# One load queue in place of two, and a rearranged token mixer, in a lightning-attention kernel on one core

## The chip, the cores and the metric

The kernel runs on one core of a Trainium2 chip. The metric is the device time of one execution in microseconds (us), and I quote medians of several executions. A ratio is the mean time of one kernel's fast runs over the mean of the other kernel's fast runs of the same rounds on the same chip, so it is not quite the ratio of the two medians. An execution over 1.5% above the fastest of the same kernel counts as slow and is left out of ratios. The profile is of one execution; its span is 1.7 us (after) to 2.0 us (before) shorter than the time of that execution (119.18 and 129.39 us). The kernel before was run again beside every experiment, with medians of 127.45 to 129.03 us, so a difference below 1% between runs of different rounds says nothing by itself.

The engines are TensorE (PE for matmuls, PEld for its weight loads), VectorE (DVE), ScalarE (ACT), GpSimd (POOL) and SyncE (SP), which here only issues DMAs.

## The reference

Four batches of eight heads, 768 positions, head width 64. First a causal linear attention with a decay per head, then a token mixer with a hidden width of 64:

```python
# per head, blocks of 64 positions
intra = (qb @ kb.T) * Dmask;  out = intra @ vb + (qb * lam_pow) @ kv_state
kv_state = lam_block * kv_state + (kb * rev_pow).T @ vb
# x: [4, 768, 512], the heads side by side
wq = x @ w_q;  wk = x @ w_k                # 512 -> 64 each
W_tok = (wq @ wk.T) / sqrt(64)
out = maximum(W_tok @ x, 0) @ w_out        # 512 -> 512
```

The kernel takes the mixer as wq @ (wk.T @ x), so no 768 x 768 matrix is made.

## The kernel before

It works on 16 pairs of heads, four pairs a batch. For a pair it loads q, k and v, scales v by a decay (GpSimd, tile `vn`), transposes q and k on TensorE (`turn`, tiles `trq` and `trk`), makes states (`dps`), scores (`sc`), the share from the states and the values (`oa`). A batch's mixer runs during the pairs of the next batch. Its first product is `pq`, the transposes for the second are `pk`, the second `py`, the third `pm` with the ReLU in its eviction (the copy of a result out of PSUM, the memory that TensorE's products are written to; tile `rmT`), and the output product `po`.

The loads: k and q are cast to bf16 by DMAs that GpSimd issues, v comes as f32 by SP.

```python
def load_kv(n):
    t = stage.tile([128, 2, NCH, D], F32, tag="fv", name="fv")
    nc.sync.dma_start(out=t, in_=v[...])
    t = stage.tile([128, 2, NCH, D], BF16, tag="fk", name="fk")
    nc.gpsimd.dma_start(out=t, in_=k[...])
# load_q: likewise, nc.gpsimd, BF16
```

The loop (AHEAD = 7, pools of nine stage buffers a tile):

```python
for n in range(N):
    load_kv(n + AHEAD); load_q(n + AHEAD)
    cast(n + 2)                      # GpSimd: vn = v * decay
    if n == 1: cast_weights()        # GpSimd
    scores(n)
    # mixer of batch b-1: mix_pk at kk 1, mix_pm(half 0) at kk 2, mix_pm(half 1) at kk 3
    turn(n + 1); flip(n - 1)
    # mix_pq at kk 0, mix_py at kk 1; two output tiles in kk 2 and 3, one in kk 0 and 1
    inter(n); values(n); states(n + 1)
```

GpSimd takes its instructions in program order, and these are both the scaling and the issuing of loads.

Of the kernel before, what the change touches and what calls it, by code (L numbers as in the profile page):

```python
# [22 lines left out]
AHEAD = 7  # L23
# [3 lines left out]
def kernel(  # L27
# [15 lines left out]
    nat = ctx.enter_context(tc.tile_pool(name="nat", bufs=3))  # L43
    tsb = ctx.enter_context(tc.tile_pool(name="tsb", bufs=3))
# [16 lines left out]

    def load_q(n):
        b, kk = pairs[n]
        t = stage.tile([128, 2, 3, 2 * D], BF16, tag="fq", name="fq")
        nc.gpsimd.dma_start(  # L65
            out=t,
            in_=q[b, 2 * kk : 2 * kk + 2].rearrange("h (a p r) d -> p h a (r d)", p=128, r=2),
        )
        staged[n, "q"] = t

    def load_kv(n):
        b, kk = pairs[n]
        t = stage.tile([128, 2, NCH, D], F32, tag="fv", name="fv")
        nc.sync.dma_start(
            out=t, in_=v[b, 2 * kk : 2 * kk + 2].rearrange("h (c p) d -> p h c d", p=128)
        )
        staged[n, "v"] = t
        t = stage.tile([128, 2, NCH, D], BF16, tag="fk", name="fk")
        nc.gpsimd.dma_start(  # L79
            out=t, in_=k[b, 2 * kk : 2 * kk + 2].rearrange("h (c p) d -> p h c d", p=128)  # L80
        )
        staged[n, "k"] = t

    lam_all = consts.tile([128, H], F32, name="lam_all")
    nc.sync.dma_start(out=lam_all, in_=lam.partition_broadcast(128))
    load_kv(0)
    load_q(0)
    load_kv(1)


# [18 lines left out]
    )  # L109
    lnl = consts.tile([128, H], F32, name="lnl")  # L110
# [16 lines left out]
    Dq = []  # L127
    for kk in range(NP):
        t = consts.tile([128, S], BF16, name=f"dq{kk}")
        nc.scalar.activation(out=t, in_=ET, func=ACT.Exp, scale=lncol[:, kk : kk + 1])  # L130
        Dq.append(t)
    maskc = consts.tile([128, 3, CH], BF16, name="maskc")

    def build_mask():
        nc.gpsimd.memset(maskc, 1.0)
        nc.gpsimd.affine_select(
            out=maskc.rearrange("j c (r p) -> j c r p", r=2),
            in_=maskc.rearrange("j c (r p) -> j c r p", r=2),
            compare_op=ALU.is_ge,
            fill=0.0,  # L140
            base=0,
            pattern=[[0, 3], [1, 2], [2, 64]],
            channel_multiplier=-1,
        )

    wqk_f = consts.tile([128, 4, 2 * DHY], F32, name="wqk_f")
    wqk = consts.tile([128, 4, 2 * DHY], BF16, name="wqk")
    wo_f = consts.tile([128, 4, HD], F32, name="wo_f")
    wo = consts.tile([128, 4, HD], BF16, name="wo")

    def load_weights():
        nc.sync.dma_start(
            out=wqk_f[:, :, 0:DHY], in_=moe_w_q.rearrange("(kt p) j -> p kt j", p=128)
        )
        nc.sync.dma_start(
            out=wqk_f[:, :, DHY:], in_=moe_w_k.rearrange("(kt p) j -> p kt j", p=128)
        )
        nc.sync.dma_start(out=wo_f, in_=moe_w_out.rearrange("(kt p) j -> p kt j", p=128))

    def cast_weights():  # L160
        nc.gpsimd.tensor_scalar_mul(
            out=wqk[:, :, 0:DHY], in0=wqk_f[:, :, 0:DHY], scalar1=1.0 / 8.0
        )
        nc.gpsimd.tensor_copy(out=wqk[:, :, DHY:], in_=wqk_f[:, :, DHY:])
        nc.gpsimd.tensor_copy(out=wo, in_=wo_f)
# [5 lines left out]
    def cast(n):  # L171
        b, kk = pairs[n]
        fk, fv = staged.pop((n, "k")), staged.pop((n, "v"))
        kn = fk
# [130 lines left out]
    def flip(n):  # L305
# [4 lines left out]
        nc.vector.tensor_copy(out=xnat[b][:, :, kk * CH : (kk + 1) * CH], in_=xp)  # L310


    M = {}

    def mix_pq(b):
        qkT = hyp.tile([128, S], BF16, tag="qkT", name="qkT")
# [159 lines left out]
```

## Time and profile before

| | before |
|---|---|
| median (first 3 runs) | 128.13 us (127.66 to 128.55) |
| span of the profiled execution | 127.4 us |
| states of pair 4 start | 43.35 us |
| one steady batch (pairs 8 to 11) | 22.2 us |
| tail after the last pair | 18.5 us (108.9 to 127.4) |

Besides the lines that the prediction shows, more readings matter. First the page itself: busy time of each engine, then the DMA issues (count, KB each, median us from issue to landing).

```profile
span 127.4 us, 3311 instructions
PE 94.8 (74%) x1382; PEld 63.3 (50%) x1392; DVE 54.8 (43%) x119; ACT 66.9 (53%) x123; POOL 59.3 (47%) x61
...
fv<-in_v_dram SPq DMA_DIRECT2D x16, 384.0 KB, 14.4
...
fk<-in_k_dram POOLq DMA_DIRECT2D x16, 192.0 KB, 20.2
fq<-in_q_dram POOLq DMA_DIRECT2D x16, 192.0 KB, 20.2
```

No engine is full over the whole span, and a load takes 14 to 20 us to land, five to seven times the 2.95 us that TensorE needs for a pair without mixer work.

Then the waits of the kernel before (engine, tile and line; what it waited for; us in total, times, longest):

```profile
PE trq L191 <- DMA fq<-in_q_dram: 16.4, 3, 9.8
...
POOL fk L79 <- DMA fk<-in_k_dram: 9.9, 7, 2.8
...
PE dps L223 <- POOL vn L176: 8.1, 3, 4.6
...
PE py L344 <- DVE wkn L338: 2.6, 3, 0.9
```

TensorE loses 24.5 us to q that has not landed and v that is not scaled. The mixer's own wait is 2.6.

Last the DMA view of 20 to 25 us (packets of each queue; q0 is GpSimd's, q1 SP's):

```profile
DMA packets 3802, 0.82 MB, mean 164 GB/s; under 512 B 3801, under 2 KB 3801, under 8 KB 3801
...
q0 software_dynamic: 1923, 0.33, 81.5%
q1 hardware_dynamic: 1878, 0.48, 72.4%
```

The two queues get equal numbers of packets in these 5 us, 760 a us together (over 10 to 45 us it is 15366 and 11683, with SP at times having less asked for). But a pair needs 2304 rows of q and k (q0) and only 1536 of v (q1), so with equal turns v runs ahead of the q and k that it is useless without: v of pair 5 lands at 33.6 us, its q at 39.5.

### The profile page before, as it was taken

The numbers are of one execution on the slowest core, as the hardware profiler recorded it, in microseconds if no ns is written. First come the engines' busy times: TensorE is split into PE (matmuls) and PEld (weight loads), VectorE is DVE, ScalarE is ACT, GpSimd is POOL, SyncE is SP. The second block draws the span as 40 slices with busy tenths as digits, with TensorE's granted clock in tenths as the row PEclk, the third lists the DMA queues.
The fourth block names the chain that finished last, engine by engine and source line by source line (L and its number), as shares of the span: only waits on it lengthen the run. The fifth ranks groups of instructions, "written<-read, shape, count | busy, mean of one in ns | idle before, by whom it ended". The sixth has DMA issues, their size and how long they took to land.

```text
span 127.4 us, 3311 instructions
## 1 busy us (share of the span) xinstructions
PE 94.8 (74%) x1382; PEld 63.3 (50%) x1392; DVE 54.8 (43%) x119; ACT 66.9 (53%) x123; POOL 59.3 (47%) x61
## 2 busy tenths in 40 slices
PE   0008290650986399799999799999979999899970
PEld 0007280530874376568586556658655665434420
DVE  0103626110658090938855919385491936110000
ACT  4292050140055025369867449786744978647970
POOL 6999963237499956675848574314040000000000
PEclk9999999555599658999999999999999999999999
DMA  2999999999999999999999999998020240424284
GB/s 44 214 166 215 215 308 167 163 164 164 162 163 165 163 164 164 163 165 164 163 163 165 182 237 206 217 219 210 16 87 0 82 153 24 157 86 161 87 331 165
DMA packets 67407, 20.41 MB, mean 160 GB/s; under 512 B 63808, under 2 KB 63808, under 8 KB 67392
## 3 DMA queue, kind: packets, MB, share of 16 engines
q0 software_dynamic: 37376, 6.29, 62.6%
q1 hardware_dynamic: 30016, 13.90, 52.5%
q8 instruction: 11, 0.18, 0.5%
q14 instruction: 4, 0.03, 0.1%
HBM read 20.19 MB, written 6.29 MB: 208 GB/s over the span
## 4 chain that ended last, share of the span: by engine, by line
PE 54%; POOL 18%; DMA 16%; DVE 4%; issue 4%; ACT 2%; POOLq 0%; ACTq 0%
PE po L373 14%; DMA fk<-in_k_dram 14%; POOL fk L79 5%; PE pq L321 5%; POOL vn L176 5%; PE py L344 5%; PE sc L245 4%; PE dps L223 4%; PE oa L289 4%; PE pm L359 4%; POOL fq L65 4%; PE oa L268 4%; PE xp L309 4%; DVE pr L257 4%; PE trq L191 3%
## 5 line engine op out<-in xcount | busy, mean ns | idle before, releaser
L257 DVE TENSOR_TENSOR pr<-sc,maskc 128x384 bf16<-128x384 f32 x64 | 31.1, 548 | 0.2 <-PE sc L245 0.2
L210 ACT COPY kT<-trk 128x768 bf16<-128x768 bf16 x16 | 12.9, 809 | 31.4 <-PE trk L206 31.4
L176 POOL TENSOR_TENSOR vn<-fv,DvI 128x768 bf16<-128x768 f32 x16 | 23.7, 1482 | 12.3 <-PE oa L289 8.5
L232 DVE CAST gs<-dps 128x320 bf16<-128x320 f32 x16 | 7.9, 492 | 37.0 <-PE dps L223 37.0
L373 PE MATMUL po<-wo,rmT 128*128 128x512 bf16 x86 | 22.5, 380 | 0.6 <-issue 0.2
L191 PE MATMUL trq<-ident,fq 128*64 128x128 bf16 x192 | 10.0, 250 | 16.4 <-DMA fq<-in_q_dram 16.4
L79 POOL DMA_DIRECT2D fk<-in_k_dram x16 | 17.1, 1071 | 10.9 <-DMA fk<-in_k_dram 9.9
L297 ACT CAST xT<-oa 128x384 bf16<-128x384 f32 x32 | 16.7, 592 | 3.2 <-PE oa L289 2.3
L65 POOL DMA_DIRECT2D fq<-in_q_dram x16 | 13.3, 830 | 10.7 <-DMA fq<-in_q_dram 3.6
L381 ACT COPY osb<-po 128x512 f32<-128x512 f32 x24 | 14.0, 601 | 7.1 <-PE po L373 5.1
L191 PEld LDWEIGHTS <-fq 128*64 128x64 bf16 x192 | 7.2, 126 | 19.3 <-DMA fq<-in_q_dram 16.9
L223 PE MATMUL dps<-vn,fk 128*64 128x320 bf16 (+4 forms) x160 | 10.7, 269 | 8.1 <-POOL vn L176 8.1
L373 PEld LDWEIGHTS <-rmT 128*128 128x128 bf16 x96 | 8.8, 98 | 10.5 <-issue 1.2
L223 PEld LDWEIGHTS <-fk 128*64 128x64 bf16 x160 | 9.0, 122 | 9.0 <-issue 8.5
L366 ACT ACTIVATE rmT<-pm 128x384 bf16<-128x384 f32 x32 | 13.0, 506 | 0.8
L197 DVE TENSOR_TENSOR qT<-trq,dq 128x768 bf16<-128x768 bf16 x16 | 8.8, 550 | 10.4 <-PE trq L191 10.4
L310 DVE COPY xnat<-xp 128x768 bf16<-128x768 bf16 x16 | 8.8, 550 | 3.5 <-PE xp L309 3.4
L206 PE MATMUL trk<-ident,fk 128*64 128x128 bf16 x192 | 9.9, 248 | 0.0
L309 PE MATMUL xp<-ident,xT 128*128 128x128 bf16 x96 | 9.1, 235 | 0.6 <-ACT xT L297 0.5
L289 PE MATMUL oa<-pr,vn 128*64 128x128 bf16 x192 | 9.3, 234 | 0.0
L245 PE MATMUL sc<-qT,kT 64*128 64x128 bf16 x192 | 9.1, 234 | 0.1
L206 PEld LDWEIGHTS <-fk 128*64 128x64 bf16 x192 | 8.0, 131 | 0.0
(35 smaller groups left out, 81.0 us busy)
## 6 DMA issues: line engine op xcount, KB each, us to landing
fv<-in_v_dram SPq DMA_DIRECT2D x16, 384.0 KB, 14.4
out_dram<-osb SPq DMA_DIRECT2D x24, 256.0 KB, 2.4
fk<-in_k_dram POOLq DMA_DIRECT2D x16, 192.0 KB, 20.2
fq<-in_q_dram POOLq DMA_DIRECT2D x16, 192.0 KB, 20.2
wo_f<-in_moe_w_out_dram SPq DMA_DIRECT2D x1, 1024.0 KB, 9.6
wqk_f<-in_moe_w_q_dram SPq DMA_DIRECT2D x1, 128.0 KB, 10.0
wqk_f<-in_moe_w_k_dram SPq DMA_DIRECT2D x1, 128.0 KB, 8.8
lam_all<-in_lam_dram SPq DMA_DIRECT2D x1, 4.0 KB, 3.2
```

Source lines behind the costliest of these rows:

```text
L65: nc.gpsimd.dma_start(out=t, in_=q[b, 2 * kk : 2 * kk + 2].rearrange("h (a p r) d -> p h a (r d)", p=128, r=2),)
L79: nc.gpsimd.dma_start(out=t, in_=k[b, 2 * kk : 2 * kk + 2].rearrange("h (c p) d -> p h c d", p=128))
L176: nc.gpsimd.tensor_tensor(out=vn, in0=fv, in1=DvI[:, 2 * kk : 2 * kk + 2, :].unsqueeze(3).to_broadcast([128, 2, NCH, D]), op=ALU.mult,)
L191: nc.tensor.transpose(trq[hl * 64 : hl * 64 + 64, a, r, :], fq[:, hl, a, r * D : (r + 1) * D], ident,)
L206: nc.tensor.transpose(trk[hl * 64 : hl * 64 + 64, c * CH : (c + 1) * CH], kn[:, hl, c, :], ident)
L223: nc.tensor.matmul(dps[hl * 64 : hl * 64 + 64, c:, :], kn[:, hl, c, :], vn[:, hl, c, :].unsqueeze(1).to_broadcast([128, m, D]), start=(c = ...
L245: nc.tensor.matmul(sc[a, hl][:, cc, :], kT[r, c * CH : (c + 1) * CH], qchunk(n, r, c), start=True, stop=True, skip_group_check=True,)
L257: nc.vector.tensor_tensor(out=t, in0=sc[a, hl], in1=maskc, op=ALU.mult)
L289: nc.tensor.matmul(oa[a][r, cc, :], vn[:, hl, c, :], pr[a, hl][:, cc, :], start=False, stop=(cc == 2), skip_group_check=True,)
L297: nc.scalar.copy(out=xT[b][:, kk, a * HALF : (a + 1) * HALF].rearrange("d (c p r) -> d c r p", c=3, r=2), in_=oa[a].rearrange("d c (r p) - ...
L309: nc.tensor.transpose(xp[:, t, :], xT[b][:, kk, t * CH : (t + 1) * CH], ident)
L373: nc.tensor.matmul(po, M[b]["rmT"][:, kt, t * CH : (t + 1) * CH], wo[:, kt, :], start=(kt == 0), stop=(kt == 3),)
```

## The change

The intent: all of q, k, v and the weights come in bf16 by casting DMAs on GpSimd's queue, in the order of need (only k and v of pair 0 come by SP); GpSimd's weight casts go; the look-ahead falls from seven pairs to five; the transposes of a pair are made two pairs ahead, behind the states; the mixer's first two products stand closer together, and the third product puts its two halves of positions on the two halves of TensorE's rows. Smaller changes go with it: VectorE scales v of pair 0, the constants are made in another order, and the pools of `vn` and of the transposed tiles grow from three buffers to four. The diff, cut to its core:

```diff
-AHEAD = 7
+AHEAD = 5
...
     def load_kv(n):
-        t = stage.tile([128, 2, NCH, D], F32, tag="fv", name="fv")
-        nc.sync.dma_start(out=t, in_=v[...])
-        t = stage.tile([128, 2, NCH, D], BF16, tag="fk", name="fk")
-        nc.gpsimd.dma_start(out=t, in_=k[...])
+        for nm, src in (("k", k), ("v", v)):
+            t = stage.tile([128, 2, NCH, D], BF16, tag="f" + nm, name="f" + nm)
+            nc.gpsimd.dma_start(out=t, in_=kv_rows(n, src))
...
-    def load_weights():   # SP, f32, three DMAs
-    def cast_weights():   # GpSimd: wq / 8, wk, wo to bf16
+    def load_wqk():       # GpSimd DMAs, cast: wq | wk | wq
+    def load_wo():        # GpSimd DMA, cast
...
-    def mix_pm(b, n):
-        for dd in range(4):
+    def mix_pm(b, dd):
+        for n in range(2):
+            r = slice(n * 64, n * 64 + 64)
             nc.tensor.matmul(pm,
-                M[b]["Y"][:, dd * CH : (dd + 1) * CH],
-                M[b]["qkT"][0:64, n * HALF : (n + 1) * HALF], ...)
-            nc.scalar.activation(out=..., in_=pm, func=ACT.Relu)
+                M[b]["Y"][r, dd * CH : (dd + 1) * CH],
+                M[b]["qkT"][r, n * HALF : (n + 1) * HALF], ...)
+            nc.scalar.activation(out=..., in_=pm, func=ACT.Relu, scale=1.0 / 8.0)
...
+    scale_v(0); load(2); turn(0); states(0); ...; scale_v(1)
+    load(3); turn(1); load_wqk(); load(4)
     for n in range(N):
-        load_kv(n + AHEAD); load_q(n + AHEAD); cast(n + 2)
+        load(n + AHEAD)
+        if n == 1: load_wo()
+        scale_v(n + 2)
         scores(n)
-        # mix_pk at kk 1, mix_pm halves at kk 2 and kk 3, turn(n + 1)
+        # all eight mix_pm at kk 2
         ...
-        done = {0: [(2, 2)], 1: [(2, 3)], 2: [(2, 4), (2, 5)], 3: [(1, 0), (1, 1)]}[kk]
+        done = {0: [(2, 4), (2, 5)], 1: [], 2: [(1, 0)], 3: [(1, 1), (1, 2), (1, 3)]}[kk]
         inter(n); values(n); states(n + 1)
+        turn(n + 2)
+        # mix_pk at kk 0
```

To feed the two row halves, the first product is given the weights as wq, wk, wq, so that wq's result lands on rows 0 to 63 for the first half of positions and on rows 64 to 127 for the second; the second product writes its result twice, one copy on each row half.

More of the change, by code (lines that the diff above doesn't have):

```diff
@@ L42 @@
     stage = ctx.enter_context(tc.tile_pool(name="stage", bufs=9))
-    nat = ctx.enter_context(tc.tile_pool(name="nat", bufs=3))
-    tsb = ctx.enter_context(tc.tile_pool(name="tsb", bufs=3))
+    nat = ctx.enter_context(tc.tile_pool(name="nat", bufs=4))
+    tsb = ctx.enter_context(tc.tile_pool(name="tsb", bufs=4))
     prb = ctx.enter_context(tc.tile_pool(name="prb", bufs=8))
@@ L58, with q_rows, kv_rows, load @@
     staged = {}
+    def q_rows(n):
+        b, kk = pairs[n]
+        return q[b, 2 * kk : 2 * kk + 2].rearrange("h (a p r) d -> p h a (r d)", p=128, r=2)
+    def kv_rows(n, src):
+        b, kk = pairs[n]
+        return src[b, 2 * kk : 2 * kk + 2].rearrange("h (c p) d -> p h c d", p=128)
     def load_q(n):
-        b, kk = pairs[n]
         t = stage.tile([128, 2, 3, 2 * D], BF16, tag="fq", name="fq")
-        nc.gpsimd.dma_start(
-            out=t,
-            in_=q[b, 2 * kk : 2 * kk + 2].rearrange("h (a p r) d -> p h a (r d)", p=128, r=2),
-        )
+        nc.gpsimd.dma_start(out=t, in_=q_rows(n))
         staged[n, "q"] = t
     def load_kv(n):
-        b, kk = pairs[n]
-        t = stage.tile([128, 2, NCH, D], F32, tag="fv", name="fv")
-        nc.sync.dma_start(
-            out=t, in_=v[b, 2 * kk : 2 * kk + 2].rearrange("h (c p) d -> p h c d", p=128)
-        )
-        staged[n, "v"] = t
-        t = stage.tile([128, 2, NCH, D], BF16, tag="fk", name="fk")
-        nc.gpsimd.dma_start(
-            out=t, in_=k[b, 2 * kk : 2 * kk + 2].rearrange("h (c p) d -> p h c d", p=128)
-        )
-        staged[n, "k"] = t
+        for nm, src in (("k", k), ("v", v)):
+            t = stage.tile([128, 2, NCH, D], BF16, tag="f" + nm, name="f" + nm)
+            nc.gpsimd.dma_start(out=t, in_=kv_rows(n, src))
+            staged[n, nm] = t
+    def load(n):
+        load_q(n)
+        load_kv(n)
+    load_q(0)
     lam_all = consts.tile([128, H], F32, name="lam_all")
     nc.sync.dma_start(out=lam_all, in_=lam.partition_broadcast(128))
-    load_kv(0)
-    load_q(0)
-    load_kv(1)
+    k0 = consts.tile([128, 2, NCH, D], F32, name="k0")
+    nc.sync.dma_start(out=k0, in_=kv_rows(0, k))
+    v0 = consts.tile([128, 2, NCH, D], F32, name="v0")
+    nc.sync.dma_start(out=v0, in_=kv_rows(0, v))
     nc.scalar.preload_act_table_set("natural_log_exp_and_others")
@@ L109 @@
     )
+    load(1)
+    maskc = consts.tile([128, 3, CH], BF16, name="maskc")
+    nc.vector.memset(maskc, 1.0)
+    nc.gpsimd.affine_select(
+        out=maskc.rearrange("j c (r p) -> j c r p", r=2),
+        in_=maskc.rearrange("j c (r p) -> j c r p", r=2),
+        compare_op=ALU.is_ge,
+        fill=0.0,
+        base=0,
+        pattern=[[0, 3], [1, 2], [2, 64]],
+        channel_multiplier=-1,
+    )
+    swap = consts.tile([128, 128], BF16, name="swap")
+    nc.vector.tensor_copy(out=swap[:, 0:64], in_=ident[:, 64:128])
+    nc.vector.tensor_copy(out=swap[:, 64:128], in_=ident[:, 0:64])
     lnl = consts.tile([128, H], F32, name="lnl")
@@ L126 @@
     nc.scalar.activation(out=DvI, in_=pw48, func=ACT.Exp, scale=-1.0)
-    Dq = []
-    for kk in range(NP):
-        t = consts.tile([128, S], BF16, name=f"dq{kk}")
-        nc.scalar.activation(out=t, in_=ET, func=ACT.Exp, scale=lncol[:, kk : kk + 1])
-        Dq.append(t)
-    maskc = consts.tile([128, 3, CH], BF16, name="maskc")
-    def build_mask():
-        nc.gpsimd.memset(maskc, 1.0)
-        nc.gpsimd.affine_select(
-            out=maskc.rearrange("j c (r p) -> j c r p", r=2),
-            in_=maskc.rearrange("j c (r p) -> j c r p", r=2),
-            compare_op=ALU.is_ge,
-            fill=0.0,
-            base=0,
-            pattern=[[0, 3], [1, 2], [2, 64]],
-            channel_multiplier=-1,
-        )
@@ L146 @@
-    wqk_f = consts.tile([128, 4, 2 * DHY], F32, name="wqk_f")
-    wqk = consts.tile([128, 4, 2 * DHY], BF16, name="wqk")
-    wo_f = consts.tile([128, 4, HD], F32, name="wo_f")
-    wo = consts.tile([128, 4, HD], BF16, name="wo")
-    def load_weights():
-        nc.sync.dma_start(
-            out=wqk_f[:, :, 0:DHY], in_=moe_w_q.rearrange("(kt p) j -> p kt j", p=128)
-        )
-        nc.sync.dma_start(
-            out=wqk_f[:, :, DHY:], in_=moe_w_k.rearrange("(kt p) j -> p kt j", p=128)
-        )
-        nc.sync.dma_start(out=wo_f, in_=moe_w_out.rearrange("(kt p) j -> p kt j", p=128))
@@ L160, in cast_weights, with make_dq @@
-    def cast_weights():
-        nc.gpsimd.tensor_scalar_mul(
-            out=wqk[:, :, 0:DHY], in0=wqk_f[:, :, 0:DHY], scalar1=1.0 / 8.0
-        )
-        nc.gpsimd.tensor_copy(out=wqk[:, :, DHY:], in_=wqk_f[:, :, DHY:])
-        nc.gpsimd.tensor_copy(out=wo, in_=wo_f)
+    Dq = [consts.tile([128, S], BF16, name=f"dq{kk}") for kk in range(NP)]
+    def make_dq(kk):
+        nc.scalar.activation(out=Dq[kk], in_=ET, func=ACT.Exp, scale=lncol[:, kk : kk + 1])
+    wqk = consts.tile([128, 4, 3 * DHY], BF16, name="wqk")
@@ L168, with scale_v @@
+    wo = consts.tile([128, 4, HD], BF16, name="wo")
+    def load_wqk():
+        for at, w in ((0, moe_w_q), (1, moe_w_k), (2, moe_w_q)):
+            nc.gpsimd.dma_start(
+                out=wqk[:, :, at * DHY : (at + 1) * DHY],
+                in_=w.rearrange("(kt p) j -> p kt j", p=128),
+            )
+    def load_wo():
+        nc.gpsimd.dma_start(out=wo, in_=moe_w_out.rearrange("(kt p) j -> p kt j", p=128))
     L = {}
     xT, xnat = {}, {}
-    def cast(n):
+    def scale_v(n):
         b, kk = pairs[n]
-        fk, fv = staged.pop((n, "k")), staged.pop((n, "v"))
-        kn = fk
@@ L175, in cast @@
         vn = nat.tile([128, 2, NCH, D], BF16, tag="vn", name="vn")
-        nc.gpsimd.tensor_tensor(
+        if n == 0:
+            kn = nat.tile([128, 2, NCH, D], BF16, tag="kn", name="kn")
+            nc.vector.tensor_copy(out=kn, in_=k0)
+            fv, eng = v0, nc.vector
+        else:
+            kn = staged.pop((n, "k"))
+            fv, eng = staged.pop((n, "v")), nc.gpsimd
+        eng.tensor_tensor(
             out=vn,
@@ L322, in mix_pq @@
                     pq,
-                    wqk[:, kt, :],
+                    wqk[:, kt, n * DHY : n * DHY + 128],
                     xT[b][:, kt, n * HALF : (n + 1) * HALF],
@@ L331, in mix_pk @@
         qkT = M[b]["qkT"]
-        pk = pst([128, NCH, DHY], BF16, "pk")
+        pk = pst([128, NCH, CH], BF16, "pk")
         for t in range(NCH):
             nc.tensor.transpose(
-                pk[:, t, :], qkT[64:128, t * CH : (t + 1) * CH], ident[64:128, 64:128]
+                pk[:, t, :], qkT[:, t * CH : (t + 1) * CH], swap if t < 3 else ident
             )
-        wkn = hyp.tile([128, NCH, DHY], BF16, tag="wkn", name="wkn")
-        nc.vector.tensor_copy(out=wkn, in_=pk)
+        wkn = hyp.tile([128, NCH, 2, DHY], BF16, tag="wkn", name="wkn")
+        nc.vector.tensor_copy(
+            out=wkn, in_=pk[:, :, 0:DHY].unsqueeze(2).to_broadcast([128, NCH, 2, DHY])
+        )
         M[b]["wkn"] = wkn
     def mix_py(b):
-        py = pst([DHY, HD], F32, "py")
+        py = pst([128, HD], F32, "py")
         for t in range(NCH):
@@ L345, in mix_py @@
                 py,
-                M[b]["wkn"][:, t, :],
+                M[b]["wkn"][:, t, :, :].rearrange("p i j -> p (i j)"),
                 xnat[b][:, t, :],
@@ L350, in mix_py @@
             )
-        Y = hyp.tile([DHY, HD], BF16, tag="Y", name="Y")
+        Y = hyp.tile([128, HD], BF16, tag="Y", name="Y")
         nc.scalar.copy(out=Y, in_=py)
@@ L360, in mix_pm @@
                 pm,
-                M[b]["Y"][:, dd * CH : (dd + 1) * CH],
-                M[b]["qkT"][0:64, n * HALF : (n + 1) * HALF],
+                M[b]["Y"][r, dd * CH : (dd + 1) * CH],
+                M[b]["qkT"][r, n * HALF : (n + 1) * HALF],
                 start=True,
@@ L366, in mix_pm @@
             nc.scalar.activation(
-                out=M[b]["rmT"][:, dd, n * HALF : (n + 1) * HALF], in_=pm, func=ACT.Relu
+                out=M[b]["rmT"][:, dd, n * HALF : (n + 1) * HALF],
+                in_=pm,
+                func=ACT.Relu,
+                scale=1.0 / 8.0,
             )
@@ L382, in mix_po @@
         nc.sync.dma_start(out=out[b, t * CH : (t + 1) * CH, :], in_=osb)
-    build_mask()
-    load_q(1)
-    cast(0)
-    for n in range(2, AHEAD):
-        if n == 3:
-            load_weights()
-        load_kv(n)
-        load_q(n)
-        if n == 2:
-            turn(0)
-            states(0)
-            cast(1)
+    make_dq(0)
+    scale_v(0)
+    load(2)
+    turn(0)
+    states(0)
+    make_dq(1)
+    make_dq(2)
+    make_dq(3)
+    scale_v(1)
+    load(3)
+    turn(1)
+    load_wqk()
+    load(4)
     for n in range(N):
@@ L400 @@
         if n + AHEAD < N:
-            load_kv(n + AHEAD)
-            load_q(n + AHEAD)
+            load(n + AHEAD)
+        if n == 1:
+            load_wo()
         if n + 2 < N:
-            cast(n + 2)
-        if n == 1:
-            cast_weights()
+            scale_v(n + 2)
         scores(n)
-        if b >= 1 and kk == 1:
-            mix_pk(b - 1)
         if b >= 1 and kk == 2:
-            mix_pm(b - 1, 0)
-        if b >= 1 and kk == 3:
-            mix_pm(b - 1, 1)
-        if n + 1 < N:
-            turn(n + 1)
+            for dd in range(4):
+                mix_pm(b - 1, dd)
         if n >= 1:
@@ L421 @@
             mix_pq(b - 1)
-        if b >= 1 and kk == 1:
-            mix_py(b - 1)
-        done = {0: [(2, 2)], 1: [(2, 3)], 2: [(2, 4), (2, 5)], 3: [(1, 0), (1, 1)]}[kk]
+        done = {0: [(2, 4), (2, 5)], 1: [], 2: [(1, 0)], 3: [(1, 1), (1, 2), (1, 3)]}[kk]
         for back, t in done:
@@ L427 @@
                 mix_po(b - back, t)
+        if b >= 1 and kk == 1:
+            mix_py(b - 1)
         inter(n)
@@ L432 @@
             states(n + 1)
+        if n + 2 < N:
+            turn(n + 2)
+        if b >= 1 and kk == 0:
+            mix_pk(b - 1)
     bl = B - 1
@@ L435 @@
     mix_pq(bl)
-    mix_po(bl - 1, 2)
+    mix_po(bl - 1, 4)
     mix_pk(bl)
-    mix_po(bl - 1, 3)
+    mix_po(bl - 1, 5)
     mix_py(bl)
-    mix_po(bl - 1, 4)
-    mix_po(bl - 1, 5)
-    mix_pm(bl, 0)
-    mix_pm(bl, 1)
+    for dd in range(4):
+        mix_pm(bl, dd)
     for t in range(NCH):
```

## The prediction

> **What bounds the kernel now.** I read the slices of the page first, then the chain of waits in order of time, then GpSimd's timeline where that chain sits, then the busy time by stretch. The slices (each about 3.2 us) show two regimes.
>
> ```profile
> PE   0008290650986399799999799999979999899970
> POOL 6999963237499956675848574314040000000000
> PEclk9999999555599658999999999999999999999999
> ```
>
> Up to about the fourteenth slice TensorE has holes and half its clock in places; after it TensorE is nearly full. The chain agrees: until 43.35 us it is GpSimd and DMA, from there on TensorE.
>
> ```profile
> 41.81 1.50 POOL vn L176
> 43.31 0.04 issue
> 43.35 1.01 PE dps L223 x9
> ...
> 65.18 0.44 PE sc L245 x12
> 65.62 0.46 PE trq L191 x12
> 66.07 0.34 PE trk L206 x12
> 66.41 0.44 PE xp L309 x6
> 66.85 1.30 PE pq L321 x8
> ...
> 69.01 0.40 PE oa L268 x10
> 69.41 0.46 PE oa L289 x12
> 69.86 0.41 PE dps L223 x10
> ```
>
> The piece at 43.35 is the state product of pair 4 (of 16), released by its scaled v. So pairs 0 to 3, with no mixer work, took 43 us, though one pair is only 2.95 us of TensorE (0.44+0.46+0.34+0.44+0.40+0.46+0.41, the warm pieces above). GpSimd's timeline says why:
>
> ```profile
> 14.47 1.03 POOL L79 DMA_DIRECT2D fk<-in_k_dram  x1
> ...
> 20.26 1.02 POOL L79 DMA_DIRECT2D fk<-in_k_dram  x1 [2.10 <-DMA fk<-in_k_dram]
> ...
> 27.35 1.02 POOL L79 DMA_DIRECT2D fk<-in_k_dram  x1 [2.78 <-DMA fk<-in_k_dram]
> 29.46 0.82 POOL L65 DMA_DIRECT2D fq<-in_q_dram  x1 [1.09 <-DMA fq<-in_q_dram]
> 30.30 1.48 POOL L176 TENSOR_TENSOR vn<-fv,DvI 128x768 bf16<-128x768 f32 x1
> ```
>
> In program order the scaling of pair 2 stands behind the loads up to pair 7. Each GpSimd load from the ninth on waits for the landing of the one eight before it (the built program has eight landing semaphores for this queue), and a landing took 20.2 us at the median, because the SP queue's v loads, up to eight more, share the engines. The scaling got its turn only at 30.30.
>
> The busy time by stretch (columns: us, then PE, PEld, DVE, ACT, POOL busy, clock, DMA share, GB/s):
>
> ```profile
> 22.00:35.00 13.00, 6.86 (x99) 5.66 (x100) 3.23 (x7) 1.83 (x3) 5.63 (x6) 0.50 1.66 163
> 43.40:65.20 21.80, 20.88 (x345) 14.90 (x347) 13.50 (x29) 12.68 (x25) 13.87 (x13) 0.87 1.60 164
> 65.20:87.40 22.20, 21.13 (x347) 14.09 (x350) 13.38 (x29) 15.48 (x31) 11.01 (x10) 1.00 1.52 202
> 109.30:127.40 18.10, 13.81 (x70) 6.01 (x71) 0.91 (x2) 10.18 (x22) 0.00 (x0) 1.00 0.42 157
> ```
>
> The third row is a steady batch: 22.2 us, TensorE 95% busy, DVE and ACT with room. The last row is the tail, with no pair left to hide it.
>
> **What the Trainium skill says.** (1) "DMA: Bandwidth & Descriptors", section "SWDGE vs HWDGE vs iDMA": a cast in a DMA is possible only from GpSimd, whose cores write the descriptors in software. The trace agrees that this costs GpSimd time: 1.07 us for k (1536 rows), 0.83 us for q (768). (2) The same page, section "Queues, rings and completion order": each engine goes round-robin over the queues that have work. That fits the 20.2 us landings: in the steady stretch the two queues get nearly equal packets. (3) "TensorE: Matmul & The Clock Gate", "Part 1": the clock is halved when idle and comes back after some 3.4 us of activity. The trace has 0.50 from 22 to 35 us. (4) "TensorEngine Tiling (Array Packing)", "PSUM Bottleneck": tiling speeds TensorE, not the emptying of PSUM. The third product is exactly this: its eight evictions ran back to back in 3.18 us in the tail (116.93 to 120.11), its eight matmuls take 1.30.
>
> **Part by part: the loads.** One queue instead of two. How fast is it alone? Between 6.4 and 9.0 us nearly all packets are GpSimd's (2307 of 2503):
>
> ```profile
> DMA packets 2503, 0.43 MB, mean 165 GB/s; under 512 B 2503, under 2 KB 2503, under 8 KB 2503
> ```
>
> That is 963 packets a us. A pair has 1536+1536+768 = 3840 packets before and after (the cast halves bytes, not rows), so 4.0 us a pair. In 40 to 44 us, with both queues mixed, it was 3080 packets in 4 us, or 5.0 us a pair. So I expect the single queue no slower, and landings in the order of need.
>
> GpSimd pays: 0.83+1.07+1.07 = 2.97 us for a pair's issues, plus 1.48 for the scaling, 4.45 us a pair against 3.38 before. At the start the order is: q0 from 1.3 to 2.5; constants to 4.1; pair 1 to 7.1; mask to 7.7; pair 2 to 10.7. Pair 1's 3840 packets cannot finish before about 6.5+4.0 = 10.5 us (pair 0's k and v, 3072 rows on SP, go first), landing about 11.5, so scaling of pair 1 runs to 13.0. Then pair 3, three weight pieces (about 0.75 each, an estimate from the two issue times above: 512 rows), pair 4, pair 5: 2.97 x 3 + 2.25 = 11.2, to 24.2; the scaling of pair 2 still stands behind all of these, to 25.7. Landings eight back should be in by then (pair 3 about 19, weights 21). Then pair 6, the output weight (0.7), scaling of pair 3: 30.9. Pair 7 and scaling of pair 4: **35.4**, against 43.31 before. That is 7.9 us gained. The weight casts on GpSimd (0.88+0.40+1.89) vanish in this sum.
>
> **The pairs on TensorE.** The transposes are two pairs ahead, behind the states; same count, same 0.80 us. The gain is that nothing waits for their copies. The wait for the scores' masks and the second product's copy (0.66 us a batch: 70.73 to 72.99 less 1.6 us of transposes in between) should go, because the copy now comes a whole iteration earlier.
>
> **The mixer.** First product 1.30 unchanged. Second product 1.41 unchanged (twice the output rows, same columns). Its transposes about 0.3. Third product: the two halves on different rows can overlap, 1.30 to 0.65 us of TensorE. But all eight evictions now come in one iteration. At 0.40 us each, after a kT copy ending 0.9 us into it, the seventh (needed by the first output product) ends at about 3.75 us. Without that wait the iteration would be 4.5 us; with it: 3.75 + 0.22 (last matmul) + 0.86 (inter and values) + 0.41 + 0.80 = 6.0.
>
> One steady batch then: first iteration 2.95 + 1.30 + 0.30 + 2 x 0.86 (two output tiles) = 6.3; second 2.95 + 1.41 = 4.4; third 6.0; fourth 2.95 + 3 x 0.86 = 5.5. Sum **22.2 us**, the same as the 22.2 measured before: the halved third product and the vanished wait pay for the new wait for ACT. GpSimd needs 4 x 4.45 = 17.8 in this time, ACT about 15.5, DVE about 14: TensorE remains the bound.
>
> **The sum.** States of pair 4 start at 35.4; 1.2 us later (states and transposes) batch 1 begins, at 36.6. Batch 1 lacks two output tiles: 22.2 - 1.7 = 20.5, to 57.1. Batch 2: 79.3. Batch 3 lacks two rounds of transposes: 20.6, to 99.9. The tail: two output tiles fewer between second and third product (1.83 less the 0.7 that TensorE then waits for Y), but the outputs wait for seven evictions instead of four (+1.2): no change, 18.1. End at 118.0 us of span; the median time was 0.7 above the span: **118.7 us**. Batch 1 at the full clock (0.87 before) is inside this sum.
>
> **Rivals.** (a) GpSimd or the queue becomes the bound throughout: v's issue adds 1.07 us a pair, and eight landing semaphores now cover 2.7 pairs, not four. If a pair took 6 us, pair 15 would be scaled near 35.4 + 66 = 101, and the end near 123 to 126. For: all GpSimd work stands in line. Against: 4.0 us of packets and 4.45 us of GpSimd are below the 5.5 us that TensorE takes. (b) The third iteration loses more: evictions at their full 0.51 us, or PSUM banks held (scores four, third product eight, eight in all). One us in each of three batches, and in the tail: 122. (c) The start goes better: TensorE is warm early and the landings lead, pair 4 ready at 31 to 32 us: 115. (d) The start stays cold and in line: pair 4 at 40: 123.
>
> **Range and chances.** The start is the larger uncertainty (31 to 40 us), the steady batch the smaller (about 1 us each). Together I take 113.0 to 124.5 for 8 in 10. Faster by over 2% means below 125.6: 0.91; within 2%: 0.07; slower: 0.02.
>
> **What would show it.** Right: the scaling of pair 4 ends near 35 us and GpSimd waits little for landings before it; landings well under 20.2 us; batches 22 us apart with TensorE over 90% busy; in each third iteration TensorE waits 1 to 2 us on the evictions; no wait of the second product on its copy. Wrong: GpSimd waiting on landings all through (rival a), gaps before the states in batches 1 to 3, a packet rate below 963 a us with one queue, or a tail that differs from 18 us by over 2.

## The result

| | before | after |
|---|---|---|
| median of 4 runs | 128.34 us (127.66 to 128.63) | 119.25 us (119.17 to 119.51) |
| span of the profile | 127.4 | 117.5 |
| pair 4 scaled | 43.31 | 35.65 |
| first scores of pairs 4, 8, 12 | 44.3, 65.1, 87.3 | 36.9, 57.2, 78.9 |
| last transposes of the output (`xp`) begin | 108.9 | 99.5 |

The ratio is 0.930 (95% interval 0.926 to 0.935): faster by 7%. Of the span's 9.9 us, 7.6 are there when the states of pair 4 start. (The profiled execution of the kernel before took 129.39 us, 1.1 more than the median; by the medians the gain is 9.1 us.)

The slices of the kernel after (each 2.9 us, in tenths) answer to those in the prediction:

```profile
PE   0046992009988999799999988999999898976960
...
POOL 5994799999999999999999996240000000000000
PEclk9999999555799999999999999999999999999998
```

TensorE is full from the tenth slice, and half clock fills three slices and part of a fourth. GpSimd is now full from the sixth to the twenty-fourth slice. The page and the DMA issues:

```profile
span 117.5 us, 3292 instructions
...
fq<-in_q_dram POOLq DMA_DIRECT2D x16, 192.0 KB, 5.9
fk<-in_k_dram POOLq DMA_DIRECT2D x15, 192.0 KB, 6.4
fv<-in_v_dram POOLq DMA_DIRECT2D x15, 192.0 KB, 6.7
```

A load lands after some 6 us in place of 14 to 20. The DMA view of the same 20 to 25 us as before:

```profile
DMA packets 5483, 0.79 MB, mean 158 GB/s; under 512 B 5483, under 2 KB 5483, under 8 KB 5483
...
q0 software_dynamic: 5483, 0.79, 226.3%
```

In these 5 us one queue moves 1097 packets a us where two moved 760. The landed bytes a second are nearly the same (158 against 164 GB/s): v's rows land as half as many bytes.

GpSimd's timeline, where it had stood waiting before (start, length, line, operation; a bracket would name a wait before it):

```profile
31.21 0.92 POOL L72 DMA_DIRECT2D fq<-in_q_dram  x1
32.09 1.05 POOL L78 DMA_DIRECT2D fk<-in_k_dram  x1
33.10 1.06 POOL L78 DMA_DIRECT2D fv<-in_v_dram  x1
34.12 1.53 POOL L179 TENSOR_TENSOR vn<-fv,DvI 128x768 bf16<-128x768 bf16 x1
```

There is no bracket: GpSimd goes from issue to issue, 4.33 us a pair (34.12 less 29.79, the scaling before). The scaling of pair 4 ends at 35.65 because it stands behind the loads up to pair 7, and for no other reason: its v had landed at 26.6. The waits of the kernel after:

```profile
PE dps L226 <- POOL vn L179: 7.9, 2, 7.6
PE trq L194 <- DMA fq<-in_q_dram: 7.5, 1, 7.5
...
POOL vn L179 <- DMA fv<-in_v_dram: 3.3, 2, 2.3
PE po L384 <- ACT rmT L374: 2.8, 9, 0.4
```

The wait for q (16.4 us before) is now only the 7.5 at the very start. The wait for scaled v is as long as before (7.9 against 8.1): 7.6 of it is for pair 2, whose scaling ends at 26.3, behind the loads up to pair 5. This is what the change left at the start. The second product's wait is gone and the output product has one of the same size, 2.8. The four iterations of the steady batch and the tail, by stretch (us, then PE, PEld, DVE, ACT, POOL busy, clock, DMA share, GB/s):

```profile
57.20:63.40 6.20, 6.15 (x97) 4.18 (x96) 3.71 (x8) 4.26 (x8) 6.20 (x8) 1.00 1.94 209
63.40:67.60 4.20, 4.15 (x84) 2.95 (x84) 3.48 (x8) 2.15 (x4) 4.20 (x5) 1.00 1.85 238
67.60:73.50 5.90, 5.17 (x89) 3.20 (x90) 3.43 (x8) 5.51 (x12) 4.92 (x5) 1.00 2.26 168
73.50:78.90 5.40, 5.35 (x89) 3.49 (x89) 3.35 (x8) 3.61 (x6) 1.50 (x2) 1.00 0.61 173
...
99.50:117.50 18.00, 11.95 (x65) 5.22 (x66) 1.11 (x2) 9.75 (x20) 0.00 (x0) 0.97 0.36 132
```

Only in the third iteration is TensorE not full (5.17 of 5.90), and there ACT is (5.51): it holds the eight evictions of the third product. The profile's chain of waits breaks off 10 us before the end in this kernel, so I read nothing from it.

### The profile page after: what moved, and what is told of

Read it like the earlier page. It is cut to its first block, busy times and chain, and to the rows that moved or that the text cites. A ratio compares the mean times of both kernels' runs of the same rounds, so it can differ in the third digit from the quotient of the medians.

```text
span 117.5 us, 3292 instructions
## 1 busy us (share of the span) xinstructions
PE 90.8 (77%) x1380; PEld 60.1 (51%) x1392; DVE 60.2 (51%) x124; ACT 67.6 (58%) x123; POOL 71.0 (60%) x74
## 5 line engine op out<-in xcount | busy, mean ns | idle before, releaser
L179 POOL TENSOR_TENSOR vn<-fv,DvI 128x768 bf16<-128x768 bf16 x15 | 22.6, 1510 | 7.2 <-PE oa L292 3.9
L384 PE MATMUL po<-wo,rmT 128*128 128x512 bf16 x87 | 23.0, 380 | 3.2 <-ACT rmT L374 2.8
L78 POOL DMA_DIRECT2D fv<-in_v_dram x15 | 15.7, 1049 | 0.0
L78 POOL DMA_DIRECT2D fk<-in_k_dram x15 | 15.6, 1041 | 0.0
L226 PE MATMUL dps<-vn,fk 128*64 128x320 bf16 (+4 forms) x150 | 9.2, 254 | 7.9 <-POOL vn L179 7.9
L194 PE MATMUL trq<-ident,fq 128*64 128x128 bf16 x192 | 9.3, 237 | 7.5 <-DMA fq<-in_q_dram 7.5
L72 POOL DMA_DIRECT2D fq<-in_q_dram x16 | 14.4, 898 | 0.8 <-POOLq L468 0.8
L226 PEld LDWEIGHTS <-fk 128*64 128x64 bf16 x150 | 7.9, 113 | 8.7 <-issue 8.2
L292 PE MATMUL oa<-pr,vn 128*64 128x128 bf16 x192 | 10.3, 228 | 1.1 <-DVE pr L260 0.7
L292 PEld LDWEIGHTS <-vn 128*64 128x64 bf16 x192 | 6.7, 112 | 3.7 <-issue 2.1
```

The costliest lines, as they stand in the source:

```text
L72: nc.gpsimd.dma_start(out=t, in_=q_rows(n))
L78: nc.gpsimd.dma_start(out=t, in_=kv_rows(n, src))
L179: eng.tensor_tensor(out=vn, in0=fv, in1=DvI[:, 2 * kk : 2 * kk + 2, :].unsqueeze(3).to_broadcast([128, 2, NCH, D]), op=ALU.mult,)
L194: nc.tensor.transpose(trq[hl * 64 : hl * 64 + 64, a, r, :], fq[:, hl, a, r * D : (r + 1) * D], ident,)
L226: nc.tensor.matmul(dps[hl * 64 : hl * 64 + 64, c:, :], kn[:, hl, c, :], vn[:, hl, c, :].unsqueeze(1).to_broadcast([128, m, D]), start=(c = ...
L292: nc.tensor.matmul(oa[a][r, cc, :], vn[:, hl, c, :], pr[a, hl][:, cc, :], start=False, stop=(cc == 2), skip_group_check=True,)
```

## The experiments

Twelve kernels ran; all gave correct results. Unless said otherwise the profile read is that of a fast execution.

**Which half of the change does it?** The first run keeps the changed kernel's loads and GpSimd order, but the mixer and the loop of before; the second is the converse.

```diff
 e1_loads_only, against the changed kernel:
-    mix_pq, mix_pk, mix_py, mix_pm, the loop and the tail of after
+    those of before (turn(n + 1), mix_pk at kk 1, mix_pm halves at kk 2 and 3)
 e2_compute_only, against the kernel before:
-    mix_pq, mix_pk, mix_py, mix_pm, the loop and the tail of before
+    those of after; nat and tsb pools of 4; GpSimd casts wq a second time
```

> The loads, constants and GpSimd order of the kernel after, with the mixer and the loop of the kernel before. Theory A (the start carries nearly all of the gain; the new mixer and the earlier transposes bring 1 to 2 us): 119.5 to 121.5 us, states of pair 4 at 35 to 37 us, a steady batch of about 22.2 us. Rival B (half of the gain is the rearranged mixer): 123 to 125 us.

> The loads and GpSimd order of the kernel before, with the mixer and the loop of the kernel after. Theory A: 126 to 128.5 us, states of pair 4 still at about 43 us, a steady batch of 21.7. Rival B: 122 to 125 us.

The loads alone (with the order of constants, the scaling of pair 0 and the pools that came with them) gave 119.34 us (118.5 to 119.45), ratio 0.930: the whole gain. The span is 117.5, that of the changed kernel. The new mixer and loop are worth nothing beside the new loads. The sum is made up so: the start gives 7.8 us (scores of pair 4 at 36.5 against 44.3), and 2.1 more come in the first iteration of batch 1, which runs at the full clock in the changed kernel too. The busy time by stretch of pair 4's iteration, the kernel before first, then this run:

```profile
44.30:50.70 6.40, 6.40 (x87) 4.53 (x86) 3.40 (x7) 2.24 (x5) 3.61 (x5) 0.63 1.62 164
```

```profile
36.50:40.80 4.30, 4.30 (x86) 3.24 (x84) 3.28 (x7) 2.31 (x5) 4.30 (x5) 1.00 2.24 168
```

The same work takes 6.4 us at a mean clock of 0.63 and 4.3 at the full clock. So the wait for pair 4 cost twice: once as idle time, and once as half clock after it.

The second run surprised me: 136.27 us (134.79 to 137.41), ratio 1.060, where I had expected a small gain or none. Its profile is of a slow execution (137.4), so I use it for the kind of wait, not for its size. The timeline shows ACT, then SP, at 65 to 79 us:

```profile
77.54 0.58 ACT L388 COPY osb<-po 128x512 f32<-128x512 f32 x1 [4.78 <-DMA out_dram<-osb]
```

```profile
65.63 5.82 SPq L389 DMA_DIRECT2D out_dram<-osb  x3
71.55 0.43 SPq L74 DMA_DIRECT2D fv<-in_v_dram  x1
72.79 5.70 SPq L389 DMA_DIRECT2D out_dram<-osb  x2
```

ACT waits 4.8 us for an output buffer, and TensorE's scores then wait 5.2 us for ACT. SP issues outputs and v in one program order, there are four output buffers, and in the new loop three output tiles follow each other in one iteration. In the changed kernel SP has only outputs after pair 0. I did not separate this from the other thing that the new loop asks for, data one pair earlier. What is shown is that the new loop on the old loads loses 7.8 us: it needs the new loads and earns nothing with them.

**Place in GpSimd's line, or landings?** The kernel before with one number changed: the scaling then stands behind fewer loads, and both queues stay.

```diff
-AHEAD = 7
+AHEAD = 4
```

> The kernel before with one constant changed: loads run 4 pairs ahead instead of 7. v still comes as f32 over SP, so two queues stay. Theory C (the start was lost because the scaling of a pair stood behind loads waiting for landings, so the order alone matters): states of pair 4 at 30 to 34 us and 115 to 119 us in all. Rival D (the two mixed queues' slow landings are the bound, so one queue is needed): pair 4 at 40 us or later and over 125 us.

It took 123.4 us (123.08 to 123.98), ratio 0.964, between the two theories. Pair 4 was scaled at 32.4, earlier than in the changed kernel. But then TensorE stops for the next pair's q:

```profile
34.91 0.51 PE L245 MATMUL sc<-qT,kT 64*128 64x128 bf16 x12
38.88 0.85 PE L191 MATMUL trq<-ident,fq 128*64 128x128 bf16 x12 [3.46 <-DMA fq<-in_q_dram]
```

So half of the gain is to be had by one constant, and the rest needs the data to land sooner. This corrects the picture in the prediction, which named the place in line as the cause.

**Does v have to come by the same queue?** The changed kernel, with v of pairs 1 to 15 as f32 by SP:

```diff
-            t = stage.tile([128, 2, NCH, D], BF16, tag="f" + nm, name="f" + nm)
-            nc.gpsimd.dma_start(out=t, in_=kv_rows(n, src))
+            dt, eng = (BF16, nc.gpsimd) if nm == "k" else (F32, nc.sync)
+            t = stage.tile([128, 2, NCH, D], dt, tag="f" + nm, name="f" + nm)
+            eng.dma_start(out=t, in_=kv_rows(n, src))
```

> The kernel after with the v of pairs 1 to 15 loaded as f32 over SP, all else as it is. GpSimd then issues two loads a pair instead of three, the two queues mix again. Theory E (the start of the kernel after is bound by GpSimd's own issue time, about 7.3 us of v issues before the scaling of pair 4): scaling of pair 4 ends at 29 to 32 us, 114 to 117 us in all. Rival D (mixed queues land late): scaling of pair 4 no earlier than 36 us, 119 us or more, with GpSimd waiting on landings.

126.91 us (median of four, one of them slow; fast runs 126.51 to 126.98), ratio 0.990: nearly all the gain is lost, although GpSimd has 1.04 us a pair less to issue. Neither theory had the mechanism whole: the scaling of pair 4 was not late (it ended at 33.5 in the profiled execution, a slow one), k was. My next theory was that nine v buffers let SP run far ahead, and that four would cure it, here and in the kernel before with a look-ahead of four:

```diff
+    stv = ctx.enter_context(tc.tile_pool(name="stv", bufs=4))    # fv from stv
```

> The kernel of the run with v over SP (126.9 us), with v's landing buffers cut from nine to four, so SP cannot run more than about four pairs ahead. Theory F (v, asked for up to nine pairs ahead, takes every second turn of the DMA engines from the q and k that are needed next; the rate is enough): 117 to 121 us, pair 4's k landed by 31 us instead of 34.2. Rival G (two mixed queues move too few packets a us, whatever their order): 124 us or more.

> The kernel before with loads 4 pairs ahead (123.4 us) and, in addition, v's landing buffers cut from nine to four. Theory F: 119 to 121.5 us, no wait of TensorE on q after the first three. Rival G: 123 to 124 us, no change against the 123.4.

126.85 us (126.41 to 127.76), ratio 0.999, and 124.09 us (123.62 to 124.92), ratio 0.975 (verdict unclear). That theory falls: fewer buffers change nothing. The profile of the first of them, a fast run, shows what happens all the same (the DMA view of 20 to 25 us, then TensorE's longest waits for data):

```profile
DMA packets 4141, 0.81 MB, mean 162 GB/s; under 512 B 4140, under 2 KB 4140, under 8 KB 4140
```

```profile
32.42 0.85 PE L211 MATMUL trk<-ident,fk 128*64 128x128 bf16 x12 [1.91 <-DMA fk<-in_k_dram]
46.73 0.53 PE L196 MATMUL trq<-ident,fq 128*64 128x128 bf16 x12 [1.27 <-DMA fq<-in_q_dram]
49.82 0.85 PE L211 MATMUL trk<-ident,fk 128*64 128x128 bf16 x12 [2.56 <-DMA fk<-in_k_dram]
```

k of pair 4 lands at 32.4 us, when v of pair 5 has been there since 29.3. TensorE waits for k and q while v lies ready.

**Is it the cast, or the queue?** The last comparison changed both. So: the changed kernel with v as f32, on GpSimd's queue.

```diff
-            t = stage.tile([128, 2, NCH, D], BF16, tag="f" + nm, name="f" + nm)
+            t = stage.tile([128, 2, NCH, D], BF16 if nm == "k" else F32, tag="f" + nm, name="f" + nm)
```

> The kernel after, still one GpSimd queue with the same number of issues, but v lands as f32 (no cast), so 786 KB land a pair instead of 590. Theory G (two queues that alternate cost packets a us, one queue alone moves about 1090 a us whatever the type): 119 to 120.5 us, the packet rate from 20 to 25 us stays above 1000 a us. Rival I (the rate is set by the bytes that land, about 160 GB/s, so the cast is what makes a pair cheaper): about 4.9 us a pair, some 770 packets a us, 122 to 127 us.

119.99 us (119.81 to 121.01), ratio 0.943 with a wide interval (0.933 to 0.954, verdict unclear), because the runs of before scattered. The time is the changed kernel's within 1 us, so the cast is not what the gain needs. In 20 to 25 us:

```profile
DMA packets 4012, 0.93 MB, mean 185 GB/s; under 512 B 3930, under 2 KB 3930, under 8 KB 4012
```

The packet count, 802 a us against 828 with two queues (4141 in 5 us), misleads. Of these packets 82 are over 2 KB: in the trace v, uncast, moves in packets of 4096 bytes, 96 a pair, where a cast v takes 1536 packets of 128 bytes and v by SP 1536 of 256. Counted as rows of 256 bytes, the run moves 1048 a us ((3930 + 82 x 16) / 5).

The bytes can be compared, for v lands as f32 in both runs. Up to the landing of all of pair 4 this run moved 4.63 MB in 28.0 us, and the run with v by SP and four buffers 5.36 MB in 32.4: 165 GB/s both. The second had moved 0.73 MB more, which is v of pair 5 and most of v of pair 6, and at 165 GB/s these take the 4.4 us that lie between the two. So at the start the two traces fit one rate and another order of landing. The table gives the time in us by which q, k and v of a pair had all landed. The first two kernels have the old loop, the other three the new one, which transposes two pairs ahead and so needs a pair's data an iteration sooner; rows are to be compared within a loop.

| | pair 4 | pair 5 | pair 6 | time |
|---|---|---|---|---|
| before | 34.3 | 39.5 | 45.5 | 128.3 |
| before, look-ahead 4 | 32.2 | 38.8 | 44.2 | 123.4 |
| after, v by SP, four buffers | 32.4 | 36.3 | 41.0 | 126.9 |
| after, v as f32 on GpSimd's queue | 28.0 | 32.1 | 36.7 | 120.0 |
| after | 26.6 | 30.2 | 33.8 | 119.3 |

Against the changed kernel itself there is a difference of rate too. It had moved 22331 packets when pair 4 was complete at 26.6 us, the run with v by SP 25373 at 32.4. By an estimate from these counts, the 3042 packets more cost 3.9 us of the 5.8, and the lower mean rate (783 a us against 840) the other 1.9.

My expectation of this run asked for over 1000 packets a us. By packets it missed (802), by rows it held (1048). What the cast does to the rate the run can't say, since the size of the packets changed with it. Its pairs land 4.1 and 4.6 us apart, which is still under the 5.4 us that TensorE takes for a pair in a batch, so the total hardly moves.

**The third product.** In the next run all of it is on rows 0 to 63, so the halves cannot overlap; the one after leaves it on both halves and gives half of its evictions to DVE.

```diff
 e5_one_half:
-            r = slice(n * 64, n * 64 + 64)
+            r = slice(0, 64)                # and wq always on rows 0 to 63
 e7_split_evict:
-            nc.scalar.activation(out=rm, in_=pm, func=ACT.Relu, scale=1.0 / 8.0)
+            if n == 0:
+                nc.scalar.activation(out=rm, in_=pm, func=ACT.Relu, scale=1.0 / 8.0)
+            else:
+                nc.vector.tensor_scalar(out=rm, in0=pm, scalar1=1.0 / 8.0, scalar2=0.0,
+                                        op0=ALU.mult, op1=ALU.max)
```

> The kernel after with the third product on the first row half alone, for both halves of the columns, as before the change; first product's weight columns and the second product's transposes to match. Theory H (the evictions bound it, overlapping matmuls bring nothing): 119.0 to 119.7 us. Rival (overlap saves its 0.65 us a batch): 121 to 122 us.

> The kernel after with the evictions of the third product's second row half on DVE, the first half stays on ACT. Theory H (ACT's eight evictions in a row set the third iteration of each batch and the start of the outputs in the tail): about 0.4 us less in each of three batches and about 1.5 us less in the tail, 116 to 117.5 us. Rival (the outputs are bound by TensorE, or DVE's masks are delayed by as much): 118.8 us or more.

One half: 119.33 us (118.8 to 120.65) against 119.25; the ratios of the two rounds, 0.937 and 0.930, lie within their intervals. The traces settle it: the third iteration of batch 2 takes 5.92 us in both (scores from 67.56 to 73.48, and from 67.17 to 73.09), and the eight matmuls spread over 1.71 us in both. The overlap on two row halves buys nothing. Split evictions: 115.88 us (115.41 to 116.31), ratio 0.912. The timeline of the third iteration, the changed kernel first, then this one:

```profile
68.36 3.18 ACT L374 ACTIVATE rmT<-pm 128x384 bf16<-128x384 f32 x8
```

```profile
67.14 1.65 ACT L376 ACTIVATE rmT<-pm 128x384 bf16<-128x384 f32 x4
...
68.57 1.94 DVE L378 TENSOR_SCALAR rmT<-pm 128x384 bf16<-128x384 f32 x4
```

ACT's row of eight becomes four, and the output product's matmuls no longer wait for ACT one by one. The third iteration of batch 2 falls from 5.9 to 5.2 us. From the first scores of each batch, the three batches give 2.0 us together; from the scores of the last pair to the end it is 21.8 us in place of 23.0, since there no later pair hides the evictions. The remaining 0.6 of the span's 3.8 us (117.5 less 113.7) is an earlier start of pair 4.

**The next bound.** Since the scaling of pair 4 still stood in line, I moved it further forward: a look-ahead of three, with the weights' loads behind the scaling of pairs 4 and 5. The second run below adds the split evictions, and takes the third product half by half.

```diff
-AHEAD = 5
+AHEAD = 3
-    load(3); turn(1); load_wqk(); load(4)
+    turn(1)
     for n in range(N): load(n + AHEAD); scale_v(n + 2)
+        if n == 2: load_wqk()
+        if n == 3: load_wo()
```

> The kernel after with loads 3 pairs ahead instead of 5 and the weights' loads moved behind the scaling of pairs 4 and 5 in GpSimd's order. Theory C (the start is bound by what stands before the scalings in GpSimd's order): scaling of pair 4 ends at 28 to 31 us instead of 35.7, 113 to 115.5 us. Rival (the landings are the next bound right behind): scaling of pair 4 at 33 us or later, 117 us or more.

> The early scalings of the run before this one, the third product half by half instead of alternating, and its second half evicted by DVE. If the two gains add: 109.5 to 112 us. If the earlier start is lost again to landings or to half clock: 113 us or more.

118.9 us (117.68 to 120.4, unclear, ratio 0.930) and 116.33 us (115.74 to 117.81, verdict unclear too), ratio 0.911. The gain hoped for came in neither; the second fell where its expectation put a start lost again. In the first, pair 4 was scaled at 28.9 as expected, but the gain was gone later. The profile of the first is of a slow execution; TensorE's timeline of the second, a fast one, has the same waits:

```profile
32.06 0.81 PE L326 MATMUL pq<-xT,wqk 128*128 128x384 bf16 x4 [1.56 <-DMA wqk<-in_moe_w_k_dram]
...
43.59 0.53 PE L194 MATMUL trq<-ident,fq 128*64 128x128 bf16 x12 [2.08 <-DMA fq<-in_q_dram]
```

The weights came late. And GpSimd in the second run waits 11.3 us in all for v to land before it scales, and issues nothing in that time: k of pair 7 was issued at 36.3 and landed at 44.8, 7.7 us after k of pair 6. Too short a look-ahead turns the landing itself into GpSimd's wait, and that wait delays the next load.

So the last run takes the middle: the split evictions in the changed kernel's order of products, a look-ahead of four, the first product's weights in their early place, the output weight behind the scaling of pair 5.

```diff
-AHEAD = 5
+AHEAD = 4
-    load(3); turn(1); load_wqk(); load(4)
+    load(3); turn(1); load_wqk()
-        if n == 1: load_wo()             # ahead of scale_v
+        if n == 3: load_wo()             # behind scale_v
```

> The changed kernel with half of the third product's evictions on DVE (115.88 us), and with a look-ahead of four pairs in place of five: the scaling of pair 4 stands behind the loads up to pair 6, not 7; the weights of the first product keep their early place, the output weight moves behind the scaling of pair 5. Theory J (the scaling's place in GpSimd's line still sets the start, as long as the data and weights are asked for in time): pair 4 is scaled at 31.5 to 32.5 us in place of 35.1, the first scores of pairs 4 and 8 start at 32.7 to 33.7 and 52.5 to 54, and the time is 112.5 to 114. Rival K (landings are the next bound, as with a look-ahead of three): pair 4 is scaled at about 32, but TensorE then waits for q and k of pairs 5 and 6 as in the run with a look-ahead of three, scores of pair 8 start at 55 or later, and the time is 115 to 116.5.

113.17 us (112.73 to 113.56, six runs), ratio 0.891 (0.887 to 0.895): as expected, and the best of all versions, 5 to 6 us under the changed kernel (by the ratios 0.930 and 0.891, and by the medians). GpSimd's timeline and two batches by stretch:

```profile
30.29 1.51 POOL L179 TENSOR_TENSOR vn<-fv,DvI 128x768 bf16<-128x768 bf16 x1
```

```profile
33.10:53.20 20.10, 19.51 (x345) 13.24 (x344) 15.80 (x34) 12.83 (x23) 20.10 (x20) 1.00 1.93 167
53.20:74.20 21.00, 20.82 (x351) 13.81 (x350) 15.72 (x34) 14.01 (x25) 18.30 (x17) 1.00 2.01 203
```

Pair 4 is scaled at 31.8 in place of 35.65, scores start at 33.1 and 53.2, and TensorE is busy for 20.82 of the 21.00 us of the steady batch.

## Why the prediction was right

The time, 118.7 predicted and 119.25 measured, and the range held. That the two lie so close is in part luck. The working gave a span of 118.0 (117.5 measured) and added 0.7, the median of the kernel before less the span of a slower execution of it (129.39 us); the profiled execution of the changed kernel was 1.7 us longer than its span, and with that the same working gives 119.7. By its own steps:

- **The start.** Right in size and mechanism: scaling of pair 4 ends at 35.65 (predicted 35.4), GpSimd takes 4.33 us a pair (4.45), waits only 3.3 us for landings, and states begin 7.6 us earlier (7.9). Incomplete as a cause: with the old queues, the same place in line was worth only 5 us (123.4), because the next pairs' q and k were not there. The words "landings in the order of need" stand in the prediction as a side remark; the runs with v by SP, which lose nearly all the gain though pair 4 is scaled earlier (33.5 and 32.2), show that it is needed as much.
- **The packet rate.** Mis-sized: 963 a us predicted for the single queue, 1097 measured. It made no difference, since GpSimd's 4.33 us and TensorE's 5.4 us a pair were both longer than the queue's 3.5 us (3840 packets at 1097 a us). The working counted rows alone; no run with one queue contradicts that, for the 802 of v as f32 in the same queue are 1048 in rows. A reading beside it was too wide: the packets of the two queues were nearly equal from 20 to 25 us (1923 and 1878), but not over the steady stretch (9487 and 5146 from 65.2 to 87.4).
- **The steady batch.** Predicted iterations 6.3, 4.4, 6.0, 5.5 and sum 22.2; measured 6.2, 4.2, 5.9, 5.4 and 21.7. The wait of the second product went, and a wait for ACT's evictions came in its place, as said, but smaller: TensorE idles 0.73 us in the third iteration (5.90 less 5.17), where 1 to 2 were forecast. The two halves were to take 0.65 us on TensorE; in the tail the eight matmuls took 0.82, and in the third iteration, paced by the evictions, they spread over 1.71. That the mixer's part nets to nothing is shown by the run of the loads alone.
- **The tail.** Predicted 18.1, measured 18.0. The longer wait for evictions there is what the split evictions took away.
- **The Trainium skill's passages.** "TensorEngine Tiling (Array Packing)", section "PSUM Bottleneck", was borne out twice: 119.33 us without the row halves, 115.88 with the evictions on two engines. "TensorE: Matmul & The Clock Gate", "Part 1", gained weight: in the kernel before, TensorE worked without a gap from 43.4 us, but its clock stayed at half until 49.0, for 5.6 us where the prediction had taken some 3.4 from the page, and one iteration was 2.1 us longer than at the full clock.
- **The rivals.** (a) did not come: pair 15 was scaled at 79.5, far below 101. (b) and (d) did not come. (c) did not come by itself, but the last run built it: the loads up to pair 6 in place of 7 ahead of the scaling, and pair 4 ready at 31.8.

What stays open is how the loss with two queues divides into order and rate: 3.9 and 1.9 us at pair 4 are an estimate from two traces. Equal turns between queues of unequal need would let v run ahead as it does, but no run set the shares otherwise, and four buffers for v did not stop it. Also open is how the loss of the run with the new loop on old loads divides between outputs behind v loads and data needed a pair earlier.

## What to carry to other kernels

When several loads of short rows are needed together, try them in one queue in the order of need, even if a second queue stands idle and even if the one engine has more to issue; then look at what its program order puts ahead of the first piece of work that others wait for. Choose the look-ahead by trying it: too long, and the work stands behind loads nobody needs yet (119.3 and 115.9 us with five pairs); too short, and the issuing engine waits for landings before it can issue more (116.3 with three, the weights late); four gave 113.2. When a product is spread over more of TensorE, count its evictions first: here they were the bound, and giving half of them to the engine with room was worth about 3 us.

## What the Trainium skill lacked or had wrong

- "DMA: Bandwidth & Descriptors", section "Issuing engines are not separate DMA queues", says that DMAs of several engines interleave on the same 16 engines and that issuing from several saves only the time of initiating. It lacks the cost: moving v from GpSimd's queue to SP's saved 1.04 us of issuing a pair and made the kernel 7.7 us slower (126.91 against 119.25), because q and k of a pair then land behind the v of later ones.
- The same page, section "Anatomy of one DMA — SWDGE (gpsimd) path", calls descriptor generation small and variable. Here a load held GpSimd for 0.90 us (768 rows) or 1.04 us (1536 rows; 1.06 for v without the cast), and the issues up to pair 7, with the scalings in between, set the start of the scaling of pair 4 at 34.12 us.
- No page gives the rate for rows of 256 to 512 bytes by queue and cast. The runs show, in 20 to 25 us: two queues with v as f32, 760 and 828 packets a us; one queue with everything cast to bf16, 1097.
- No page says that a cast decides whether rows are joined. From GpSimd's queue, with the same access pattern, v with the cast went in 1536 packets of 128 bytes a pair, and without it in 96 of 4096 bytes.
